# Attention with a mixture of experts on one core: GpSimd's additions in pieces, relus two ahead, unit 1's second weight later, the last tile in two

## Chip, cores and metric

One core of a Trainium2 chip. The number that counts is the device time of one execution, in microseconds (us). The time before is the median of three timed runs; one more execution was profiled, and all rows below are from it.

## What is computed

```python
# q, k, v: (2, 8, 576, 64); hidden 32; moe: N=1152 tokens, D=512, E=4 experts, F=1024
scores = scale * q @ k.T + bias          # bias[h,i,j] = relu(psi*w1 + b1) @ w2, psi = log1p|i-j| / log1p(i)
attn   = softmax(scores)
x      = (attn @ v)  as (1152, 512)
p      = domain_probs / domain_probs.sum(-1)
for e in range(4):
    h    = relu(x @ w1[e])               # 1152 x 1024
    out += p[:, e] * (h @ w2[e])         # 1152 x 512
```

## The kernel before

The attention stage comes first (to about 195 us). It leaves x in SBUF as a sum of two float16 parts (`xx`, high and low), 512 features on 4 x 128 partitions by 1152 tokens. The expert stage cuts the four experts into eight units of 512 hidden columns (`NU = 8`). Each unit has a first weight (512 x 512, `m = 0`) and a second one (`m = 1`). Both are loaded as float32 in halves of 128 x 1024 (`raw`), scaled by a power of two of the largest element, and split into a high and a low float16 part: `whi` (L457, ScalarE; L459 where VectorE does it) and `wlo` (L463, VectorE) for the second weight, L577 and L578 for the first one of units 1 to 7. A product takes three matmuls per 128 rows: high by high, high by low, low by high.

Unit 0 is plain. `mm1` (L475 to L477) makes its hidden rows in three token blocks c of 384 and four column blocks ft of 128; for each, ScalarE applies the relu twice (`ev_a`: L480 into the float32 buffer `hf`, of which there are three, and L481 into the float16 `hh`), and VectorE forms the low part by a difference (`ev_v`, L484). `mm2` (L497 to L499) multiplies a tile of 128 tokens (tau 0 to 8) by the second weight, 12 matmuls of 512 columns, and `sum_up` (L504 for unit 0, L506 for the others) adds it to `acc` by the gate. I write M1.5 for mm2 of unit 1, tile 5.

Units 1 to 7 save one product in eight (seven block products in place of eight, `quad`, L594), for which sums of blocks of x and of the first weight are needed. x is put together in float32 by GpSimd (`x_whole`, L547), summed by VectorE (`x_sums`, L544) and split again (`x_halves`, L555 and L553). The weight's sums are GpSimd's (`w_sums`, L574). Each of a unit's 28 block products goes into one of four PSUM banks; VectorE adds them (L665), ScalarE copies (L685) and applies the relus (L675, L676), GpSimd forms the low part (L677). Tokens come in two pairs of 320 and 256 columns.

The largest element of a weight is found by VectorE per partition (`wmax`, L427, in halves; L436 joins two), written to memory (L439), read back to all partitions (L443) and reduced (`w_red`, L446); `wscale` is five small steps, `gate_unit` (L452) one on 128x9 elements. The outcome goes out tile by tile (`store`, L512, on SP's queue).

The order of all this is set by two planners of the class `Plan`: each step has a priority, an estimated cost, the steps that it needs (`deps`) and steps that must only stand ahead of it (`after`), and the planner writes the instructions in the order of a simulated run. On the chip each engine then takes its own instructions in that order and waits for data alone. The first planner covers the attention stage, unit 0's blocks c = 0 and 1 and the early weights (its steps for unit 1 have names with a 1 at the end, `whi1`, `wlo1`, `gate1`). The second one, `plan_experts`, covers the rest; there `weights(u)` prepares a unit's weights, `second(u, tau)` is mm2 with its sum and store.

Of the kernel before, what the change touches and what calls it, by code (L numbers as in the profile page):

```python
# [155 lines left out]
def tile_attention_moe(ctx: ExitStack, tc: tile.TileContext, qd, kd, vd, cst, ltab, dp, mw1, mw2, out):  # L156
# [328 lines left out]

    def mm2(u, tau, ps):
        if u:
            i = tau // 5
            hh, hl = hpair(i, 0), hpair(i, 1)
            ts = slice(P * (tau - 5 * i), P * (tau - 5 * i) + P)  # L490
        else:
            c, tt = divmod(tau, 3)
            hh, hl = hpart(u, c, 0), hpart(u, c, 1)
            ts = slice(P * tt, P * tt + P)
        wh, wl = wpart(u, 1, 0), wpart(u, 1, 1)
        for ft in range(4):
            T.matmul(ps, hh[:, ft, ts], wh[:, ft], start=(ft == 0), stop=False)  # L497
            T.matmul(ps, hh[:, ft, ts], wl[:, ft], start=False, stop=False)  # L498
            T.matmul(ps, hl[:, ft, ts], wh[:, ft], start=False, stop=(ft == 3))  # L499

    def sum_up(u, tau, ps):
        g, acc = gu[:, u % 2, tau:tau + 1], moe["acc"][:, tau]
# [93 lines left out]
    def plan_experts():  # L596
# [10 lines left out]
        def all_(kind, u, n):  # L607
            return [(kind, u, k) for k in range(n)] if u >= 0 else []

        def weights(u):  # L610
            at = 42.0 * u - 34 if u > 1 else 5.0
            p2, p1 = u - 2, u - 1
            for m in range(2 if u > 1 else 0):
                for j in range(2):
                    if u > 1:
                        after = [("part", p1, k) for k in range(4)] if m == 0 else [("whi", p1, j), ("wlo", p1, j)] if p1 > 1 else []
                        op(("load", u, m, j), "S", at - 10, 1.4, lambda m=m, j=j: load_w(u, m, j), deps=after)
                    prev = (all_("part", p2, 4) + ([("gate", p2)] + [("wlo", p2, k) for k in range(2)] if p2 > 1 else [])) if p2 >= 1 else []
                    op(("wmax", u, m, j), "V", at + 2 * m + j, 1.21, lambda m=m, j=j: wmax(u, m, j), deps=[("load", u, m, j)] if u > 1 else [], after=prev)
                op(("wboth", u, m), "V", at + 2 * m + 2, 0.16, lambda m=m: w_both(u, m), deps=[("wmax", u, m, j) for j in range(2)], after=[("wred", u - 1)] if u > 2 else [])  # L620
# [8 lines left out]
            for k, (c, fns) in enumerate(zip((1.15, 0.63, 0.63, 1.6), w_parts(u))):  # L629
                for e, x, fn in zip("AV", (0, 0.15 * c), fns):  # L630
                    op((("parth" if e == "A" else "part"), u, k), e, at + 12 + 3 * k, c + x, fn, deps=([("wscale", u, 0)] if u > 1 else []) + ([("wsum", u)] if k != 1 else []) + ([("parth", u, k)] if e == "V" else []), after=used)
            if u == 1:
                return
            for j in range(2):
                used2 = [("mm2", p2, tau) for tau in range(NTAU)] if p2 >= 0 else []
                op(("whi", u, j), "A", 42.0 * u - 12 + 4 * j, 1.14, lambda j=j: whi("A", u, 1, j), deps=[("wscale", u, 1)], after=used2)
                op(("wlo", u, j), "V", 42.0 * u - 11 + 4 * j, 1.28, lambda j=j: wlo("V", u, 1, j), deps=[("whi", u, j)])
            op(("gate", u), "V", 42.0 * u - 4, 0.29, lambda: gate_unit(u), deps=[("wscale", u, m) for m in range(2)], after=[("sum", p2, tau) for tau in range(NTAU)] if p2 >= 0 else [])

        def second(u, tau, at):  # L640
# [188 lines left out]
    op("wred1", (), early, w_red, 1, deps=[("wcast1",)])  # L829
    op("gate1", (), early, gate_unit, 1, deps=[("wscale1", 0), ("wscale1", 1), ("prep_gate",)])  # L830
    for c in range(2):
        for ft in range(4):
            for kt in range(4):
# [4 lines left out]
                   deps=[("xlo", 3 * c + i) for i in range(3)] + [("wlo", 0, j) for j in range(2)])  # L838
            op("ev_a", (c, ft), PR["ev"], lambda c=c, ft=ft, key=key: ev_a(0, c, ft, buf[key][:, 0:384], hf[:, (4 * c + ft) % 3]), deps=[("mm1", c, ft, 3)], use=[key], after=[("ev_v", c, ft - 1)] if ft else [("ev_v", c - 1, 3)] if c else [])
# [78 lines left out]
```

## Time and profile before

| | |
|---|---|
| median of three timed runs | 566.19 us (565.79 to 566.46) |
| the profiled execution, its time | 566.17 us |
| its span, first to last instruction | 564.4 us |
| TensorE busy | 542.4 us, 96% |
| VectorE busy | 408.4 us, 72% |
| ScalarE busy | 293.8 us, 52% |
| GpSimd busy | 146.3 us, 26% |
| mean granted TensorE clock | 0.987 of full speed |

Busy time is an average over stages that have different limits, so the table alone doesn't tell what a change is worth. It is to be read by stretches: which engine waits, for whom, and what that one was doing. A row of the timeline has the start, the length, the engine, the line, what is written and read, and in brackets the idle time before it and what ended it.

### The profile page before, as it was taken

The numbers are of one execution on the slowest core, as the hardware profiler recorded it, in microseconds if no ns is written. First come the engines' busy times: TensorE is split into PE (matmuls) and PEld (weight loads), VectorE is DVE, ScalarE is ACT, GpSimd is POOL, SyncE is SP. The second block draws the span as 40 slices with busy tenths as digits, with TensorE's granted clock in tenths as the row PEclk, the third lists the DMA queues.
The fourth block names the chain that finished last, engine by engine and source line by source line (L and its number), as shares of the span: only waits on it lengthen the run. The fifth ranks groups of instructions, "written<-read, shape, count | busy, mean of one in ns | idle before, by whom it ended". The sixth has DMA issues, their size and how long they took to land.

```text
span 564.4 us, 11030 instructions
## 1 busy us (share of the span) xinstructions
PE 542.4 (96%) x4354; PEld 341.4 (60%) x4354; DVE 408.4 (72%) x829; ACT 293.8 (52%) x611; POOL 146.3 (26%) x156
## 2 busy tenths in 40 slices
PE   8769999999999995999999999999999999999997
PEld 3236667777777852547556565665665665565753
DVE  7658887878889496887795976967958957534532
ACT  5568888787787541625534544544334533423410
POOL 0000000000000082007263471371642624322310
PEclk9799999999999997999999999999999999999999
DMA  6984332132441102021041311410312210000022
GB/s 210 235 279 136 105 122 79 62 104 71 138 148 39 11 1 74 1 75 11 14 136 11 115 35 11 149 11 17 135 10 75 75 11 1 2 1 0 1 76 93
DMA packets 22020, 40.63 MB, mean 72 GB/s; under 512 B 3024, under 2 KB 4048, under 8 KB 21968
## 3 DMA queue, kind: packets, MB, share of 16 engines
q1 hardware_dynamic: 21680, 39.33, 23.9%
q8 instruction: 34, 0.56, 0.4%
q10 hardware_dynamic: 288, 0.59, 0.3%
q14 instruction: 18, 0.15, 0.1%
HBM read 25.75 MB, written 2.37 MB: 50 GB/s over the span
## 4 chain that ended last, share of the span: by engine, by line
PE 87%; DVE 5%; DMA 4%; ACT 2%; issue 1%; SPq 0%; ACTq 0%; DVEq 0%
PE bank L594 24%; PE bank L497 11%; PE bank L499 11%; PE bank L498 11%; PE bank L350 7%; PE bank L318 7%; PE bank L335 7%; PE bank L291 5%; PE bank L361 2%; DMA biasA<-obr 1%; DMA biasB<-obr 1%; DVE hh L484 1%; DMA vv<-vd 1%; DVE wb L463 1%; PE bank L231 1%
## 5 line engine op out<-in xcount | busy, mean ns | idle before, releaser
L677 POOL TENSOR_TENSOR hp<-hf,hp 128x320 f16<-128x320 f32 (+1 forms) x112 | 92.1, 838 | 203.4 <-ACT hf L676 202.4
L594 PEld LDWEIGHTS <-wn 128*128 128x128 f16 x1176 | 115.0, 98 | 40.4 <-issue 1.7
L675 ACT ACTIVATE hp<-xsf 128x320 f16<-128x320 f32 (+1 forms) x112 | 49.0, 437 | 137.9 <-DVE xsf L665 137.4
L665 DVE SCALAR_TENSOR_TENSOR xsf<-bank,xsf 128x320 f32<-128x320 f32 (+1 forms) x196 | 82.4, 451 | 25.6 <-PE bank L594 18.4
L594 PE MATMUL bank<-xs,wn 128*128 128x320 f16 (+1 forms) x672 | 98.2, 286 | 1.0 <-ACT xsf L685 0.6
L506 DVE SCALAR_TENSOR_TENSOR acc<-bank,gu,acc 128x512 f32<-128x512 f32 x63 | 47.1, 747 | 66.9 <-PE bank L499 66.9
L594 PE MATMUL bank<-xx,wn 128*128 128x320 f16 (+1 forms) x504 | 75.5, 286 | 0.0
L330 ACT ACTIVATE er<-er,mr 128x576 f32<-128x576 f32 x72 | 55.2, 769 | 10.6 <-DVE mr L326 10.4
L286 DVE TENSOR_SCALAR fr<-lt,npt 128x576 f32<-128x576 f32 x117 | 52.9, 514 | 5.7 <-PE bank L291 5.4
L497 PE MATMUL bank<-wb,hp 128*128 128x512 f16 x144 | 54.6, 379 | 0.0
L498 PE MATMUL bank<-wb,hp 128*128 128x512 f16 x144 | 54.6, 379 | 0.0
L499 PE MATMUL bank<-wb,hp 128*128 128x512 f16 x144 | 54.6, 379 | 0.0
L318 PE MATMUL bank<-ks,qr 64*128 64x288 f32 (+1 forms) x320 | 47.2, 427 | 5.1 <-ACT obr L294 2.4
L291 PE MATMUL bank<-fr,cs 128*32 128x288 f32 x576 | 44.4, 434 | 3.8 <-ACT obr L294 3.2
L676 ACT ACTIVATE hf<-xsf 128x320 f32<-128x320 f32 (+1 forms) x112 | 47.8, 427 | 0.2 <-POOL hp L677 0.2
L339 ACT ACTIVATE etr<-bank 128x512 f32<-128x512 f32 x69 | 37.5, 596 | 16.6 <-PE bank L335 15.3
L350 PE MATMUL bank<-etr,vv 128*64 128x128 f32 (+1 forms) x800 | 45.5, 265 | 0.0
L350 PEld LDWEIGHTS bank<-etr,vv 128*64 128x64 f32 x800 | 39.6, 137 | 8.6 <-issue 6.8
L499 PEld LDWEIGHTS <-hp 128*128 128x128 f16 x252 | 24.7, 98 | 29.7
L335 PE MATMUL bank<-ident,er 128*128 128x128 f32 x324 | 42.1, 278 | 0.0
L335 PEld LDWEIGHTS bank<-ident,er 128*128 128x128 f32 x324 | 34.8, 141 | 12.0 <-issue 8.4
L497 PE MATMUL bank<-wa,hp 128*128 128x512 f16 x108 | 40.9, 379 | 0.0
(104 smaller groups left out, 763.8 us busy)
## 6 DMA issues: line engine op xcount, KB each, us to landing
raw<-mw SPq DMA_DIRECT2D x32, 512.0 KB
biasB<-obr SPq DMA_DIRECT2D x32, 144.0 KB
biasA<-obr SPq DMA_DIRECT2D x32, 144.0 KB
vv<-vd SPq DMA_DIRECT2D x8, 320.0 KB
ks<-kd SPq DMA_DIRECT2D x8, 288.0 KB
qr<-qd SPq DMA_DIRECT2D x9, 256.0 KB
biasA<-obr SPq DMA_DIRECT2D x8, 288.0 KB
out<-acc SPq DMA_DIRECT2D x8, 256.0 KB
```

Source lines behind the costliest of these rows:

```text
L286: ENG[e].tensor_scalar(out=f, in0=src, scalar1=npt[:, g:g + 1], scalar2=None, op0=ALU.max)
L291: T.matmul(buf["pb", n][32 * t:32 * t + 32, half, 0:288], W2, buf["f", n, t][:, 288 * half:288 * half + 288], start=True, stop=True)
L318: T.matmul(s_out(2 * p + h, c0, c1, half), q[r, c0:c1], ks[r, HP * b + hp, 288 * half:288 * half + 288], start=True, stop=True)
L330: A.activation(out=ehalf(u), in_=ehalf(u), func=AF.Exp, scale=-1.0, bias=buf["m", u // 2][:, u % 2:u % 2 + 1], accum_out=buf["sum", tau][: ...
L335: T.transpose(buf["t", tau, g][:, P * i:P * i + P], buf["e", HP * tau + hp][:, P * j:P * j + P], ident)
L350: T.matmul(x[64 * h:64 * h + 64, P * hp + c0:P * hp + c1], vv[:, HP * b + hp, 5 * h + i], buf["et", tau, g][:, P * j + c0:P * j + c1], sta ...
L497: T.matmul(ps, hh[:, ft, ts], wh[:, ft], start=(ft == 0), stop=False)
L498: T.matmul(ps, hh[:, ft, ts], wl[:, ft], start=False, stop=False)
L499: T.matmul(ps, hl[:, ft, ts], wh[:, ft], start=False, stop=(ft == 3))
L594: T.matmul(ps, w[lw][:, k], x[:, lx, k], start=k == 0 and lw + lx == 0, stop=k == 1 and lw == 1)
L665: V.scalar_tensor_tensor(out=tmp(name), in0=ps(a), scalar=2.0 ** -HS, in1=tmp(other), op0=ALU.mult, op1=ALU.add)
L677: op(("lo", u, i, x), "G", at + pos + EV, 0.2 + 0.6 * r, lambda: G.tensor_tensor(out=lo, in0=buf[f][:, 0:n], in1=hi, op=ALU.subtract), dep ...
```

## The change

Four edits, three of them in what the planners are told.

GpSimd's `x_whole` is cut along the four feature blocks: per token pair four instructions in place of one. In the first planner the relu pair of a block need no longer stand behind the difference just before it, but behind the one before that (a pair may be up to two ahead). Unit 1's `whi`, `wlo` and `gate_unit` leave the first planner and are made by `weights(1)` in the second one, always by ScalarE and VectorE; mm2 of unit 1 and loads of later units are told of them. The last tile's mm2, sum and store are done in two parts, of 320 and 192 columns.

```diff
-    def x_whole(i):
-        G.tensor_tensor(out=moe["xf"][:, :, tokens(i)], in0=xx[:, 0, :, tokens(i)], in1=xx[:, 1, :, tokens(i)], op=ALU.add)
+    def x_whole(i, k):
+        G.tensor_tensor(out=moe["xf"][:, k, tokens(i)], in0=xx[:, 0, k, tokens(i)], in1=xx[:, 1, k, tokens(i)], op=ALU.add)
...
-                        after = [("part", p1, k) for k in range(4)] if m == 0 else [("whi", p1, j), ("wlo", p1, j)] if p1 > 1 else []
+                        after = [("part", p1, k) for k in range(4)] if m == 0 else [("whi", p1, j), ("wlo", p1, j)]
...
-                    prev = (all_("part", p2, 4) + ([("gate", p2)] + [("wlo", p2, k) for k in range(2)] if p2 > 1 else [])) if p2 >= 1 else []
+                    prev = ([("gate", p2)] + all_("part", p2, 4) + [("wlo", p2, k) for k in range(2)]) if p2 >= 1 else []
...
-            if u == 1:
-                return
...
         def second(u, tau, at):
             i = tau // 5
+            if (u, tau) == (NU - 1, NTAU - 1):
+                for k, o in enumerate((slice(0, 320), slice(320, DM))):
+                    key = (u, tau, k)
+                    op(("mm2",) + key, "T", at, 1.3, lambda o=o, key=key: mm2(u, tau, buf[("o",) + key], o), ...
+                    op(("sum",) + key, "V", at + 2.6 + EV, 0.45, lambda o=o, key=key: sum_up(u, tau, buf[("o",) + key], o), ...
+                    op(("store",) + key, "S", at, 0.5, lambda o=o: store(tau, o), deps=[("sum",) + key])
+                return
             if u:
-                deps = [("lo", u, i, k) for k in range(8)] + ([("wlo", u, j) for j in range(2)] if u > 1 else [])
+                deps = [("lo", u, i, k) for k in range(8)] + [("wlo", u, j) for j in range(2)]
...
-            op(("xw", i), "G", 6.0 * i, 6.0 - i, lambda i=i: x_whole(i))
+            for k in range(4):
+                op(("xw", i, k), "G", 6.0 * i, 1.4 - 0.2 * i, lambda i=i, k=k: x_whole(i, k))
...
-            if m:
-                op("whi1", (j,), early, whi, 1, m, j, choice=True, deps=[("wscale1", m)])
-                op("wlo1", (j,), early, wlo, "V", 1, m, j, deps=[("whi1", j)])
...
-    op("gate1", (), early, gate_unit, 1, deps=[("wscale1", 0), ("wscale1", 1), ("prep_gate",)])
...
-            op("ev_a", (c, ft), ..., after=[("ev_v", c, ft - 1)] if ft else [("ev_v", c - 1, 3)] if c else [])
+            op("ev_a", (c, ft), ..., after=[("ev_v",) + divmod(4 * c + ft - 2, 4)] if 4 * c + ft > 1 else [])
```

What that does to the order is seen on VectorE at two places. The first is behind the scales of unit 1, while TensorE ends unit 0's first products (L484 are the differences, L452 the gate step, L459 and L463 unit 1's second weight, L504 unit 0's sums). Before:

```order
L452 TENSOR_SCALAR gu<-gate,ws 128x9
L484 TENSOR_TENSOR hh<-hf,hh 128x384
L459 TENSOR_SCALAR wb<-raw_1669,ws 128x1024
L463 SCALAR_TENSOR_TENSOR wb<-raw_1669,ws,wb 128x1024
L484 TENSOR_TENSOR hh<-hf,hh 128x384
L463 SCALAR_TENSOR_TENSOR wb<-raw_1669,ws,wb 128x1024
L484 TENSOR_TENSOR hh<-hf,hh 128x384 x4
```

Now, at the same place (L544 is a sum of x, L579 was L578):

```order
L484 TENSOR_TENSOR hh<-hf,hh 128x384 x6
L504 TENSOR_SCALAR acc<-bank,gu 128x512
L452 TENSOR_SCALAR gu<-gate,ws 128x9
L463 SCALAR_TENSOR_TENSOR wb<-raw_1669,ws,wb 128x1024
L504 TENSOR_SCALAR acc<-bank,gu 128x512
L544 TENSOR_TENSOR xsf<-xsf 128x2x320
L579 SCALAR_TENSOR_TENSOR wn<-raw,ws,wn 128x512
L504 TENSOR_SCALAR acc<-bank,gu 128x512
L544 TENSOR_TENSOR xsf<-xsf 128x2x320
L463 SCALAR_TENSOR_TENSOR wb<-raw_1669,ws,wb 128x1024
```

The six differences now stand in a row, and the second weight and the gate step have gone behind unit 0's first sum. On ScalarE eight relu pairs stand in a row in the same way; L457, which stood behind the third pair, comes twice behind the eighth.

The second place is the border from unit 1 to unit 2 on VectorE, behind unit 2's scales (L506 sums of unit 1, L578 and L463 unit 2's weights, L665 additions of unit 1). Before:

```order
L578 SCALAR_TENSOR_TENSOR wn<-raw,ws,wn 128x1024
L506 SCALAR_TENSOR_TENSOR acc<-bank,gu,acc 128x512
L578 SCALAR_TENSOR_TENSOR wn<-raw,ws,wn 128x512 x2
L506 SCALAR_TENSOR_TENSOR acc<-bank,gu,acc 128x512
L463 SCALAR_TENSOR_TENSOR wa<-raw_1669,ws,wa 128x1024
L578 SCALAR_TENSOR_TENSOR wn<-wt,ws,wn 128x1536
L665 SCALAR_TENSOR_TENSOR xsf<-bank,xsf 128x256 x3
```

Now (L579 was L578, L672 was L665):

```order
L579 SCALAR_TENSOR_TENSOR wn<-raw,ws,wn 128x1024
L463 SCALAR_TENSOR_TENSOR wa<-raw_1669,ws,wa 128x1024
L672 SCALAR_TENSOR_TENSOR xsf<-bank,xsf 128x256 x3
L506 SCALAR_TENSOR_TENSOR acc<-bank,gu,acc 128x512
L579 SCALAR_TENSOR_TENSOR wn<-raw,ws,wn 128x512 x2
L672 SCALAR_TENSOR_TENSOR xsf<-bank,xsf 128x256
L506 SCALAR_TENSOR_TENSOR acc<-bank,gu,acc 128x512
L579 SCALAR_TENSOR_TENSOR wn<-wt,ws,wn 128x1536
```

The last piece of unit 2's first weight (128x1536) has moved behind the four last additions of unit 1. Ahead of this place, unit 2's maxima of the second weight (L427 on raw_1669) have moved from unit 0's sums into unit 1's additions, and the step that reduces them (L446) from the first half of unit 1's last additions to behind two L506. On TensorE M1.5 now stands ahead of unit 2's first product, where it stood behind its fourth.

## Rows read from the trace of the kernel before

**Rows 1.** Stretch, length, busy us (count) of PE, PEld, DVE, ACT, POOL, clock, DMA, GB/s.
```profile
251.50:530.00 278.50, 277.51 (x1761) 172.09 (x1760) 199.76 (x380) 122.09 (x271) 116.41 (x128) 1.00 0.16 42
```

**Rows 2.** Waits, 196 to 222 us: who for whom, total us, times, longest.
```profile
ACT hf L480 <- DVE hh L484: 7.5, 3, 4.6
...
PE bank L497 <- ACT hh L481: 6.7, 1, 6.7
```

**Rows 3.** VectorE: all L484 (ns min/median/max); timeline start, length (us).
```profile
L484 DVE TENSOR_TENSOR hh<-hf,hh x12: 543/551/3906, 199.0 to 237.6; 128x384 f16<-128x384 f32 x12
...
200.96 3.91 DVE L484 TENSOR_TENSOR hh<-hf,hh 128x384 f16<-128x384 f32 x1 [0.24 <-ACT hh L481]
...
205.60 3.22 DVE L452 TENSOR_SCALAR gu<-gate,ws 128x9 f32<-128x9 f32 x1
```

**Rows 4.** GpSimd, timeline from 199 us.
```profile
199.32 9.47 POOL L547 TENSOR_TENSOR xsf<-xx 128x2560 f32<-128x2560 f16 x2 [9.91 <-DVE xx L380]
...
208.75 1.65 POOL L574 TENSOR_TENSOR wt<-raw 128x512 f32<-128x512 f32 x1
```

**Rows 5.** ScalarE, timeline, 205 to 218 us.
```profile
205.54 1.15 ACT L457 ACTIVATE wb<-raw,ws 128x1024 f16<-128x1024 f32 x1 [2.66 <-DVE ws L271]
...
217.47 0.49 ACT L480 ACTIVATE hf<-bank 128x384 f32<-128x384 f32 x1 [1.80 <-DVE hh L484]
...
217.85 0.48 ACT L481 ACTIVATE hh<-bank 128x384 f16<-128x384 f32 x1
```

**Rows 6.** TensorE, timeline: around the pause, and unit 1's first product.
```profile
211.39 0.33 PE L477 MATMUL bank<-xx,wa 128*128 128x384 f16 x1
...
218.39 0.59 PE L497 MATMUL bank<-wa,hh 128*128 128x512 f16 x1 [6.67 <-ACT hh L481]
...
251.50 0.98 PE L594 MATMUL bank<-xx,wn 128*128 128x320 f16 x6
```

**Rows 7.** Stretches, columns as in rows 1.
```profile
40.00:42.00 2.00, 0.15 (x6) 0.01 (x2) 2.00 (x5) 0.00 (x0) 0.00 (x0) 1.00 0.79 300
...
215.00:215.50 0.50, 0.00 (x0) 0.00 (x0) 0.50 (x1) 0.50 (x2) 0.50 (x1) 1.00 0.97 332
...
218.00:222.00 4.00, 3.61 (x9) 1.31 (x9) 0.87 (x2) 0.94 (x2) 0.00 (x0) 0.50 0.40 130
...
222.00:226.00 4.00, 4.00 (x19) 1.72 (x17) 2.77 (x4) 0.00 (x0) 0.00 (x0) 0.94 0.00 0
```

**Rows 8.** Units 1 and 2: timelines of VectorE and SP's queue; one chain row.
```profile
247.53 1.81 DVE L578 SCALAR_TENSOR_TENSOR wn<-wt,ws,wn 128x1536 f16<-128x1536 f32 x1
...
259.90 0.34 SPq L439 DMA_DIRECT2D wd<-wx  x1
...
263.35 0.34 SPq L443 DMA_DIRECT2D wg<-wd  x1
...
268.03 0.41 DVE L446 TENSOR_REDUCE ws<-wg 128x2 f32<-128x256 f32 x1
...
272.90 0.75 DVE L506 SCALAR_TENSOR_TENSOR acc<-bank,gu,acc 128x512 f32<-128x512 f32 x1 [2.17 <-PE bank L499]
...
275.49 0.75 DVE L506 SCALAR_TENSOR_TENSOR acc<-bank,gu,acc 128x512 f32<-128x512 f32 x1
...
276.16 1.41 DVE L578 SCALAR_TENSOR_TENSOR wn<-raw,ws,wn 128x512 f16<-128x512 f32 x2
...
279.94 1.81 DVE L578 SCALAR_TENSOR_TENSOR wn<-wt,ws,wn 128x1536 f16<-128x1536 f32 x1
...
284.54 3.92 PE bank L594 x30
```

**Rows 9.** Groups by form (count, busy us, mean ns, idle); one stretch.
```profile
L506 DVE SCALAR_TENSOR_TENSOR acc<-bank,gu,acc 128x512 f32<-128x512 f32 x63 | 47.1, 747 | 66.9 <-PE bank L499 66.9
...
L665 DVE SCALAR_TENSOR_TENSOR xsf<-bank,xsf 128x256 f32<-128x256 f32 x98 | 37.5, 416 | 8.9 <-PE bank L594 4.8 <-ACT xsf L685 3.6
...
562.00:563.00 1.00, 0.00 (x0) 0.00 (x0) 0.00 (x0) 0.00 (x0) 0.00 (x0) 1.00 0.70 262
```

More of the change, by code (lines that the diff above doesn't have):

```diff
@@ L496, in mm2, with sum_up @@
         for ft in range(4):
[L497 to L502, printed above, removed]
+            T.matmul(ps[:, o], hh[:, ft, ts], wh[:, ft, o], start=(ft == 0), stop=False)
+            T.matmul(ps[:, o], hh[:, ft, ts], wl[:, ft, o], start=False, stop=False)
+            T.matmul(ps[:, o], hl[:, ft, ts], wh[:, ft, o], start=False, stop=(ft == 3))
+    def sum_up(u, tau, ps, o=slice(0, DM)):
+        g, acc, ps = gu[:, u % 2, tau:tau + 1], moe["acc"][:, tau, o], ps[:, o]
         if u == 0:
@@ L506, in sum_up, with store @@
             V.scalar_tensor_tensor(out=acc, in0=ps, scalar=g, in1=acc, op0=ALU.mult, op1=ALU.add)
-    def store(tau):
-        acc = moe["acc"][:, tau]
+    def store(tau, o=slice(0, DM)):
+        acc = moe["acc"][:, tau, o]
         if tau:
             r = (tau - 1) % 2 * S + (tau - 1) // 2 * P
-            SP.dma_start(out=out[r:r + P], in_=acc)
+            SP.dma_start(out=out[r:r + P, o], in_=acc)
         else:
@@ L631, in weights @@
                     op((("parth" if e == "A" else "part"), u, k), e, at + 12 + 3 * k, c + x, fn, deps=([("wscale", u, 0)] if u > 1 else []) + ([("wsum", u)] if k != 1 else []) + ([("parth", u, k)] if e == "V" else []), after=used)
-            if u == 1:
-                return
             for j in range(2):
                 used2 = [("mm2", p2, tau) for tau in range(NTAU)] if p2 >= 0 else []
-                op(("whi", u, j), "A", 42.0 * u - 12 + 4 * j, 1.14, lambda j=j: whi("A", u, 1, j), deps=[("wscale", u, 1)], after=used2)
+                op(("whi", u, j), "A", 42.0 * u - 12 + 4 * j, 1.14, lambda j=j: whi("A", u, 1, j), deps=[("wscale", u, 1)] if u > 1 else [], after=used2)
                 op(("wlo", u, j), "V", 42.0 * u - 11 + 4 * j, 1.28, lambda j=j: wlo("V", u, 1, j), deps=[("whi", u, j)])
-            op(("gate", u), "V", 42.0 * u - 4, 0.29, lambda: gate_unit(u), deps=[("wscale", u, m) for m in range(2)], after=[("sum", p2, tau) for tau in range(NTAU)] if p2 >= 0 else [])
+            op(("gate", u), "V", 42.0 * u - 4, 0.29, lambda: gate_unit(u), deps=[("wscale", u, m) for m in range(2)] if u > 1 else [], after=[("sum", p2, tau) for tau in range(NTAU)] if p2 >= 0 else [])
         def second(u, tau, at):
             i = tau // 5
+            if (u, tau) == (NU - 1, NTAU - 1):
+                for k, o in enumerate((slice(0, 320), slice(320, DM))):
+                    key = (u, tau, k)
+                    op(("mm2",) + key, "T", at, 1.3, lambda o=o, key=key: mm2(u, tau, buf[("o",) + key], o), deps=[("lo", u, i, x) for x in range(8)] + [("wlo", u, j) for j in range(2)] + ([("mm2", u, tau - 1)] if not k else [("mm2", u, tau, 0)]), new=[("o", ("o",) + key)])
+                    op(("sum",) + key, "V", at + 2.6 + EV, 0.45, lambda o=o, key=key: sum_up(u, tau, buf[("o",) + key], o), deps=[("mm2",) + key, ("gate", u)], use=[("o",) + key], after=[("sum", u - 1, tau)])
+                    op(("store",) + key, "S", at, 0.5, lambda o=o: store(tau, o), deps=[("sum",) + key])
+                return
             if u:
-                deps = [("lo", u, i, k) for k in range(8)] + ([("wlo", u, j) for j in range(2)] if u > 1 else [])
+                deps = [("lo", u, i, k) for k in range(8)] + [("wlo", u, j) for j in range(2)]
             else:
@@ L646, in second @@
             op(("mm2", u, tau), "T", at, 2.6, lambda: mm2(u, tau, buf["o", u, tau]), deps=deps, new=[("o", ("o", u, tau))])
-            op(("sum", u, tau), "V", at + 2.6 + EV, 0.75, lambda: sum_up(u, tau, buf["o", u, tau]), deps=[("mm2", u, tau)] + ([("gate", u)] if u > 1 else []), use=[("o", u, tau)], after=[("sum", u - 1, tau)] if u else [])
+            op(("sum", u, tau), "V", at + 2.6 + EV, 0.75, lambda: sum_up(u, tau, buf["o", u, tau]), deps=[("mm2", u, tau)] + ([("gate", u)] if u else []), use=[("o", u, tau)], after=[("sum", u - 1, tau)] if u else [])
             if u == NU - 1:
@@ L699, in plan_experts @@
         for i in range(2):
-            op(("xw", i), "G", 6.0 * i, 6.0 - i, lambda i=i: x_whole(i))
+            for k in range(4):
+                op(("xw", i, k), "G", 6.0 * i, 1.4 - 0.2 * i, lambda i=i, k=k: x_whole(i, k))
             for k, fn in enumerate(x_sums(i)):
-                op(("xs", i, k), "V", 1 + 12.0 * i + k, 0.85, fn, deps=[("xs", i, k - 1)] if k else [("xw", i)])
+                op(("xs", i, k), "V", 1 + 12.0 * i + k, 0.85, fn, deps=[("xs", i, k - 1)] if k else [("xw", i, x) for x in range(4)])
             for a in range(2):
@@ L838, in tile_attention_moe @@
                    deps=[("xlo", 3 * c + i) for i in range(3)] + [("wlo", 0, j) for j in range(2)])
[L839 removed]
+            op("ev_a", (c, ft), PR["ev"], lambda c=c, ft=ft, key=key: ev_a(0, c, ft, buf[key][:, 0:384], hf[:, (4 * c + ft) % 3]), deps=[("mm1", c, ft, 3)], use=[key], after=[("ev_v",) + divmod(4 * c + ft - 2, 4)] if 4 * c + ft > 1 else [])
             op("ev_v", (c, ft), PR["ev"], lambda c=c, ft=ft: ev_v(0, c, ft, None, hf[:, (4 * c + ft) % 3]), deps=[("ev_a", c, ft)])
```

4 lines of the change are left out of this document (2 added, 2 removed).

## Prediction

> **What bounds the kernel now.** I read the table of stretches first. Behind 251.50 us, in the expert stage, TensorE is busy 277.51 of 278.50 us [rows 1]: there only a shorter product or a shorter end could help, and nothing in the change shortens a product. The list of waits then names the one large hole, at the border from unit 0's first products to its second ones: TensorE waits 6.7 us for a relu on ScalarE, and ScalarE itself waits 7.5 us, in three pieces, for VectorE's differences (L484) [rows 2]. So the question is why a difference is late. Its median is 0.551 us, its longest 3.906 us; that one runs from 200.96 to 204.87 [rows 3]. GpSimd's two additions of L547 cover 199.32 to 208.79 [rows 4]; shared out by columns (2560 and 2048) the first ends near 204.6. VectorE's gate step on 128x9 elements starts at 205.60 and ends at 208.82 [rows 3], which is where the second addition ends. My reading is that VectorE stands still until GpSimd's running instruction is over, and then gets its turn.
>
> ScalarE's order adds to it: L457 (unit 1's second weight) stands between relus and waits 2.66 us for a scale that is queued on VectorE behind the long difference, and the last relu pair waits 1.80 us for a difference [rows 5]. Its second relu ends at 218.33, and TensorE's first L497 starts at 218.39 [rows 5, 6]. TensorE had nothing to do since 211.72 (211.39 + 0.33), hence 6.67 us.
>
> **What the clock adds.** After that pause the clock is lower: 1.00 up to 215.50, 0.50 from 218 to 222, 0.94 on average from there to 226 [rows 7]. A shorter hole, 40 to 42 us with TensorE busy 0.15 us, left it at 1.00 [rows 7]. Of the two levels (1.2 and 2.4 GHz) TensorE ran at the lower one for 3.61 us (218.39 to 222) and 4 x 0.06 / 0.5 = 0.48 us, so 4.09 us in which half the work was done: 2.05 us lost.
>
> **The change, part by part.** *GpSimd's additions.* Two instructions become eight. The 9.47 us shared out by columns give 1.32 us for a piece of 640 and 1.05 for one of 512, if nothing is paid per instruction; the nearest short row, 1.65 us for 512 columns beside VectorE's steps [rows 4], gives up to 2.1 us for 640. So a difference now waits for one piece, at most 1.3 to 2.1 us, in place of up to 3.4.
>
> The Trainium skill ("SBUF — State Buffer", "Who interferes with whom") says that an operation of VectorE with both inputs in SBUF and a GpSimd instruction that reads SBUF exclude each other for a whole instruction, whoever starts first. The long difference above agrees. By the same rule VectorE holds up GpSimd as well, which speaks against many small pieces: each can be put off by a difference, and the sums of x come later.
>
> That cost has a cover. Eight differences take 8 x 0.55 = 4.4 us, so the pieces end near 199.3 + 9.5 + 4.4 = 213.2, and the first sum of x stands on VectorE behind two sum_ups of unit 0, which come some 5 us later. Cost taken: zero; with pieces at the upper price up to 1 us, since 8 x 0.5 us more still end before 218.
>
> *Relus two ahead, weights later.* Now ScalarE has eight relu pairs in a row, and a pair needs only the difference three before it (three buffers hf). TensorE ends the last group at 211.72, and the pair for it needs the fifth difference. Even if GpSimd gave VectorE no turn before all eight pieces are done (208.8), four more differences of 0.55 end at 211.0, in time; so TensorE alone releases the last pair. The two relus take 0.86 us (217.47 to 218.33 [rows 5]); with 0.1 us for the handovers TensorE goes on at 212.7. The pause falls from 6.67 to 0.97 us: **-5.70**. It can't vanish, because L497's bank is the one that the last pair reads. With pieces at the upper price it is 1.5 us.
>
> *Clock.* A pause of 0.97 us is shorter than the hole that left the clock alone: **-2.05**; at the other end of the bound, 0.
>
> *Up to unit 1's products.* VectorE loses two maxima (L427) and the cast L459 in this stretch and gains two L463 and the gate step; each but the last is one pass over 1024 columns, so its work stays about as long. ScalarE gets two casts of 1.15 us [rows 5] where it mostly waits. Before, VectorE's last piece of the weights ended at 249.34 [rows 8] and TensorE came at 251.50 [rows 6]: 2.2 us of cover, and both ends move with TensorE. GpSimd's L574 now falls beside the gate step and the first L463: at most two waits of 1.65 us, so 3.3 - 2.2 = 1.1 us at the worst. Cost taken: zero.
>
> *Border to unit 2.* Two maxima now stand between unit 1's additions, the pair of L436 comes seven additions later, and the last piece of unit 2's weights stands behind two more sum_ups and one more addition. I count from unit 1's first product (251.50). Before: M1.0's sum_up starts at 272.90 (+21.4), the next one 2.59 us later, the last piece runs to 281.75 (+30.3), and unit 2's products start behind unit 1's last one of 0.65 us, at 285.2 (+33.7) [rows 8]. After: by the count of additions the maxima are sent near +14.5; L443 follows 3.45 us later (as 263.35 follows the send at 259.90) and lands no more than 4.7 us after that (263.35 to 268.03 [rows 8]), so by +22.7. w_red stands behind the second sum_up, at +24.7, and doesn't wait. Behind it come its own 0.4, two scales of 0.6 (five small steps, what is left between 272.90 and 276.16 beside two sum_ups and a piece), a sum_up 0.7, a piece and L463 of 1.3 each, three additions 1.2, a sum_up, two pieces 1.4: about +33. The last addition waits for TensorE, +33.9, then a sum_up 0.75 and the last piece 1.8: +36.6. TensorE does M1.5 first (2.6 us, to +36.3), a product of 0.8 us, and wants the piece some 0.3 us into the next, at +37.4. Cover 0.8 us, thin. Cost taken: zero; up to 2.5 us.
>
> From unit 3 on the two orders differ by a place here and there, at the same distance to the products: zero.
>
> *End.* The last tile's 12 matmuls of 512 columns become 12 of 320 and 12 of 192, by columns the same. Its last sum_up works on 192 columns: 747 ns for 512 and 416 for 256 [rows 9] give about 0.34, so -0.41. The last store carries 98 of 262 KB; the full one moved in 1.0 us [rows 9]. In proportion that is -0.63, at a fixed price 0; I take half, -0.3, and +0.1 for TensorE's 12 more weight loads (0 to 0.35). Sum **-0.6**, from -1.0 to 0.
>
> The Trainium skill ("DMA: Bandwidth & Descriptors", "Bandwidth") advises few large transfers and shows small ones ruled by a fixed cost. No row here shows a store of 98 KB. By that advice the store saves nothing and the sum is 0.3 us higher.
>
> **Sum.** 5.70 + 2.05 + 0.6 = 8.35 us off the profiled execution's 566.17 us (span 564.4). The median of the three timed runs, 566.19, is the same. Forecast 557.8 us.
>
> **Rivals.** *A, unit 2's weights come late.* VectorE's queue ahead of the last piece is 0.8 us from deciding. For: one wait for a GpSimd instruction of 1.65 us would do. Against: VectorE waits for TensorE several times in that stretch, and these waits absorb lateness. Price 0.5 to 2.5 us, with 1.5: 559.3 us. *B, it doesn't do what it says*: relus and differences still take turns, the pause stays above 3 us and the clock falls all the same. Gain then at most 3.7 + 0.6, so about 562 us. Against stands the count above, in which even eight unbroken pieces don't put off the last relu. *C, slower.* The copy of the maxima to all partitions (L439, L443, w_red) leaves later, and w_red stands in VectorE's queue ahead of all that unit 2 needs; the additions behind it hold TensorE's four banks, so TensorE stops with it. It costs from a landing at +24.7 on, 2 us behind the latest by the trace. To undo 8.35 us and add 1.1, it must land 11 us later than that: over 567.3 us. Nothing in the trace points there.
>
> **How the numbers follow.** The forecast 0.74 (556.8 to 558.8), A 0.16, B 0.05, C 0.03, and 0.02 for a gain within 0.2%. The range runs from the best end of the tail, with the two small holes left in the expert stage closing a little, 556.8, to the upper part of A, 560.6. 0.2%, or 1.1 us, is about what a measurement here can tell from no change. Faster 0.95, same 0.02, slower 0.03.
>
> **What the next profile would show.** A pause of about 1 us before the first L497, released by a relu; clock 1.00 through it; the longest difference under 2.7 us; eight additions of GpSimd of 1.0 to 2.1 us; unit 1's products from about 243.7; no hole in TensorE at unit 2's first products; a last sum_up near 0.34 us. I am wrong if the pause stays above 2 us, if the clock reads 0.5 behind it, or if TensorE waits at unit 2 for the last piece of its weights.

## The result and the profile after

The changed kernel took 559.86 us (median of four runs, 559.28 to 561.29), against 566.24 us for the kernel before in the same comparison: a ratio of 0.9892, 95% interval 0.9873 to 0.9912. The forecast was 557.8 us in a range of 556.8 to 560.6. The direction and the range held; the forecast itself was 2 us too low, and what that was made of is told under "Right and wrong". The profiled execution took 559.86 us, with a span of 558.1 us and a mean clock of 0.991.

In the changed kernel L548 is GpSimd's addition (L547 before), L575 the weights' sums (L574), L579 the low part of the first weight (L578), L595 the products (L594), L672 the additions of products (L665), L692 their copies on ScalarE (L685), L683 the relu that GpSimd's difference reads, and L684 that difference (L677). Lines with numbers under 547 have kept them.

The list of waits of TensorE from 205 to 560 us (who for whom, total us, times, longest):

```profile
PE bank L499 <- POOL hp L684: 1.1, 1, 1.1
PE bank L497 <- ACT hh L481: 1.0, 1, 1.0
PE bank L595 <- ACT xsf L692: 0.6, 2, 0.3
PE bank L595 <- DVE xsf L672: 0.4, 2, 0.2
```

Against [rows 2] the wait of 6.7 us has shrunk to 1.0, and the first line is new. The last two were there before, at the same size. The timeline of TensorE at both stops and at unit 1's first product (start us, length, what, idle before and who ended it):

```profile
213.60 0.38 PE L497 MATMUL bank<-wa,hh 128*128 128x512 f16 x1 [0.96 <-ACT hh L481]
...
244.71 0.98 PE L595 MATMUL bank<-xx,wn 128*128 128x320 f16 x6
...
281.83 0.39 PE L499 MATMUL bank<-wb,hp 128*128 128x512 f16 x1 [1.06 <-POOL hp L684]
```

The first answers to [rows 6]: a pause of 0.96 us where 6.67 stood. The clock around it, by stretches (columns as in rows 1), answers to [rows 7]: 1.00 where 0.50 and 0.94 stood.

```profile
211.70:215.00 3.30, 2.34 (x13) 1.14 (x12) 1.97 (x2) 2.32 (x4) 3.22 (x4) 1.00 0.00 0
218.00:222.00 4.00, 4.00 (x21) 1.87 (x20) 3.41 (x5) 0.00 (x0) 0.00 (x0) 1.00 0.38 131
222.00:226.00 4.00, 4.00 (x27) 2.43 (x25) 4.00 (x6) 1.40 (x4) 0.00 (x0) 1.00 0.10 16
```

VectorE's longest difference and GpSimd's additions, to be read beside [rows 3, 4]: 3.91 us has become 1.64, and two additions of together 9.47 us have become eight of together 11.60.

```profile
201.88 1.64 DVE L484 TENSOR_TENSOR hh<-hf,hh 128x384 f16<-128x384 f32 x1 [0.24 <-ACT hh L481]
```

```profile
200.25 11.60 POOL L548 TENSOR_TENSOR xsf<-xx 128x640 f32<-128x640 f16 x8 [9.91 <-DVE xx L380]
```

**Where the new stop comes from.** It is the last product of M1.5 at the border to unit 2. GpSimd forms the last low part that M1.5 reads; VectorE works on the 128x1536 piece of unit 2's weights meanwhile. First GpSimd's last two rows, then VectorE's:

```profile
277.19 1.57 POOL L684 TENSOR_TENSOR hp<-hf,hp 128x256 f16<-128x256 f32 x2 [12.20 <-ACT hf L683]
279.70 2.08 POOL L684 TENSOR_TENSOR hp<-hf,hp 128x256 f16<-128x256 f32 x1 [0.94 <-ACT hf L683]
```

```profile
279.44 1.81 DVE L579 SCALAR_TENSOR_TENSOR wn<-wt,ws,wn 128x1536 f16<-128x1536 f32 x1
281.17 1.69 DVE L463 SCALAR_TENSOR_TENSOR wa<-raw,ws,wa 128x1024 f16<-128x1024 f32 x1
```

The piece ends at 281.25, GpSimd's difference at 281.78, and TensorE goes on at 281.83. In the kernel before the same difference took 0.67 us, since the piece was over by then, and M1.5 stood behind four products of unit 2:

```profile
286.49 0.67 POOL L677 TENSOR_TENSOR hp<-hf,hp 128x256 f16<-128x256 f32 x1 [0.95 <-ACT hf L676]
```

What the stop costs is read from unit 1's and 2's sums (L506). Here are the first one after, then the fourteenth, which is behind the border, before and after:

```profile
266.12 0.75 DVE L506 SCALAR_TENSOR_TENSOR acc<-bank,gu,acc 128x512 f32<-128x512 f32 x1 [2.17 <-PE bank L499]
```

```profile
329.46 0.74 DVE L506 SCALAR_TENSOR_TENSOR acc<-bank,gu,acc 128x512 f32<-128x512 f32 x1
```

```profile
323.90 0.74 DVE L506 SCALAR_TENSOR_TENSOR acc<-bank,gu,acc 128x512 f32<-128x512 f32 x1
```

The first one starts at 272.90 before [rows 8] and at 266.12 after, 6.78 us earlier. The fourteenth starts 5.56 us earlier. So 1.22 us are given back there, and from the fourteenth to the last sum of a whole tile nothing more.

**The end.** The last tile's two sums, and the stretches behind them, all from the changed kernel:

```profile
554.05 0.55 DVE L506 SCALAR_TENSOR_TENSOR acc<-bank,gu,acc 128x320 f32<-128x320 f32 x1 [0.88 <-PE bank L499]
555.04 0.42 DVE L506 SCALAR_TENSOR_TENSOR acc<-bank,gu,acc 128x192 f32<-128x192 f32 x1 [0.44 <-PE bank L499]
```

```profile
555.00:556.00 1.00, 0.00 (x0) 0.00 (x0) 0.42 (x1) 0.00 (x0) 0.00 (x0) 1.00 0.47 164
556.00:557.00 1.00, 0.00 (x0) 0.00 (x0) 0.00 (x0) 0.00 (x0) 0.00 (x0) 1.00 0.31 98
```

The last sum took 0.42 us in place of 0.75. From its end to the end of the span it is 2.64 us (555.46 to 558.1), against 3.09 before (561.31 to 564.4).

**A measure free of the attention stage.** The first L484 starts at 199.01 us in the profile before [rows 3] and at 199.93 after, though the instructions ahead of it are the same. In the profiles of the experiments it lies between 199.31 and 199.90. The rows show where that comes from: one product of the attention stage (L318), before and after.

```profile
48.17 1.24 PE L318 MATMUL bank<-ks,qr 64*128 64x288 f32 x8 [0.81 <-DVE sr L354]
```

```profile
49.09 1.24 PE L318 MATMUL bank<-ks,qr 64*128 64x288 f32 x8 [1.95 <-DMA qr<-qd]
```

From this row to the first L484 it is 150.84 us in both, and in the profiles of the experiments too, to 0.01 us. In the kernel before, the load of q was there in time; in the nine other profiles TensorE waits for it, and the row starts between 48.47 and 49.09. In e5, which has the instructions of the kernel before up to 212 us, it starts at 48.92. So that variation belongs to the executions, not to the change; why the load lands at different times stays open. Therefore below I compare from the start of the first L484 to the end of the span: **365.39 us before, 358.17 after, 7.22 less.** The span is given to 0.1 us, so such a difference is good to about 0.1 us. Of the sums in between, the same ones agree within 0.02 us from one kernel to another where nothing was changed.

### The profile page after: what moved, and what is told of

Same layout as the page of the kernel before. It is cut to its first block, busy times and chain, and to the rows that moved or that the text cites. A ratio compares the mean times of both kernels' runs of the same rounds, so it can differ in the third digit from the quotient of the medians.

```text
span 558.1 us, 11067 instructions
## 1 busy us (share of the span) xinstructions
PE 541.3 (97%) x4366; PEld 341.9 (61%) x4366; DVE 402.1 (72%) x829; ACT 295.0 (53%) x612; POOL 146.1 (26%) x162
## 4 chain that ended last, share of the span: by engine, by line
PE 88%; DMA 5%; ACT 3%; DVE 1%; issue 1%; POOL 1%; SPq 1%; ACTq 0%; POOLq 0%
PE bank L595 24%; PE bank L499 10%; PE bank L497 10%; PE bank L498 10%; PE bank L350 7%; PE bank L318 7%; PE bank L335 7%; PE bank L291 5%; PE bank L361 2%; PE bank L475 1%; DMA qr<-qd 1%; PE bank L477 1%; PE bank L476 1%; DMA biasB<-obr 1%; DMA biasA<-obr 1%
## 5 line engine op out<-in xcount | busy, mean ns | idle before, releaser
L684 POOL TENSOR_TENSOR hp<-hf,hp 128x320 f16<-128x320 f32 (+1 forms) x112 | 91.0, 827 | 197.2 <-ACT hf L683 194.9
L595 PEld LDWEIGHTS <-wn 128*128 128x128 f16 x1176 | 115.1, 98 | 40.5 <-issue 1.7
L672 DVE SCALAR_TENSOR_TENSOR xsf<-bank,xsf 128x320 f32<-128x320 f32 (+1 forms) x196 | 82.3, 452 | 24.2 <-PE bank L595 17.3
L595 PE MATMUL bank<-xs,wn 128*128 128x320 f16 (+1 forms) x672 | 98.0, 286 | 1.0 <-ACT xsf L692 0.6
L506 DVE SCALAR_TENSOR_TENSOR acc<-bank,gu,acc 128x512 f32<-128x512 f32 (+1 forms) x64 | 47.3, 739 | 66.7 <-PE bank L499 66.6
L595 PE MATMUL bank<-xx,wn 128*128 128x320 f16 (+1 forms) x504 | 75.5, 286 | 0.0
L499 PE MATMUL bank<-wb,hp 128*128 128x512 f16 (+2 forms) x148 | 55.2, 373 | 1.1 <-POOL hp L684 1.1
L497 PE MATMUL bank<-wb,hp 128*128 128x512 f16 (+2 forms) x148 | 55.2, 373 | 0.0
L498 PE MATMUL bank<-wb,hp 128*128 128x512 f16 (+2 forms) x148 | 55.2, 373 | 0.0
L318 PE MATMUL bank<-ks,qr 64*128 64x288 f32 (+1 forms) x320 | 46.5, 427 | 5.4 <-ACT obr L294 3.1
L291 PE MATMUL bank<-fr,cs 128*32 128x288 f32 x576 | 45.7, 445 | 3.8 <-ACT obr L294 3.2
L683 ACT ACTIVATE hf<-xsf 128x320 f32<-128x320 f32 (+1 forms) x112 | 47.8, 427 | 0.0
L497 PE MATMUL bank<-wa,hp 128*128 128x512 f16 x108 | 40.9, 379 | 0.0
```

The lines of the kernel that those rows point to most:

```text
L291: T.matmul(buf["pb", n][32 * t:32 * t + 32, half, 0:288], W2, buf["f", n, t][:, 288 * half:288 * half + 288], start=True, stop=True)
L318: T.matmul(s_out(2 * p + h, c0, c1, half), q[r, c0:c1], ks[r, HP * b + hp, 288 * half:288 * half + 288], start=True, stop=True)
L497: T.matmul(ps[:, o], hh[:, ft, ts], wh[:, ft, o], start=(ft == 0), stop=False)
L498: T.matmul(ps[:, o], hh[:, ft, ts], wl[:, ft, o], start=False, stop=False)
L499: T.matmul(ps[:, o], hl[:, ft, ts], wh[:, ft, o], start=False, stop=(ft == 3))
L595: T.matmul(ps, w[lw][:, k], x[:, lx, k], start=k == 0 and lw + lx == 0, stop=k == 1 and lw == 1)
```

## The experiments

The theory is a sum: the pause, the clock that falls behind it, the new stop at the border, and the end. Each of the four terms has a run of its own, and the last run puts three cures together. e1 to e4 ran on one chip (the kernel before there: 566.91 us) and e5 to e8 on another (566.15 us); each ratio is against these. The changed kernel was not timed again there, so an experiment is compared with it by the traces. Where a sum (L506) is said to come earlier or later, it is counted from the first L484 of the same profile.

**The relus two ahead.** This edit was not run, because there is nothing to run. The changed kernel written with the old rule for the relu pairs is the same program, instruction for instruction on every engine and with the same waits; and so is the old kernel written with the new rule. The edit does nothing by itself.

**e1, the kernel before with the eight pieces alone.**

```diff
-        G.tensor_tensor(out=moe["xf"][:, :, tokens(i)], in0=xx[:, 0, :, tokens(i)], in1=xx[:, 1, :, tokens(i)], op=ALU.add)
+        G.tensor_tensor(out=moe["xf"][:, k, tokens(i)], in0=xx[:, 0, k, tokens(i)], in1=xx[:, 1, k, tokens(i)], op=ALU.add)
```

> The kernel before with GpSimd's additions in eight pieces and nothing else of the change. Theory: VectorE waits for one running GpSimd instruction, so the longest difference (L484) falls from 3.9 to under 2.5 us, but unit 1's second weight still stands between relus and differences; the pause ahead of the first L497 falls from 6.7 to about 3.3 us (2.5 to 4.5), and the time to 561 to 563.5 us. Rival (the order of ScalarE and VectorE alone makes the pause, pieces don't matter): pause 5.5 us or more, time 565 to 566.5 us.

Measured: 561.77 us (560.32 to 563.71), ratio 0.9906 (0.9885 to 0.9927). The longest difference falls to 1.63 us, the pause to 2.48 us, and unit 1's sums come 4.50 us earlier than in the kernel before. But the clock did fall, and only when TensorE was back at work. The first L497, then the stretches:

```profile
215.09 0.38 PE L497 MATMUL bank<-wa,hh 128*128 128x512 f16 x1 [2.48 <-ACT hh L481]
```

```profile
214.00:215.00 1.00, 0.00 (x0) 0.00 (x0) 1.00 (x2) 0.84 (x3) 1.00 (x1) 1.00 0.73 268
215.00:216.00 1.00, 0.91 (x4) 0.39 (x4) 1.00 (x2) 0.64 (x2) 0.92 (x2) 0.88 0.59 225
216.00:219.00 3.00, 3.00 (x8) 1.03 (x7) 2.69 (x2) 0.00 (x0) 2.92 (x3) 0.50 0.00 0
219.00:220.00 1.00, 1.00 (x5) 0.43 (x4) 0.44 (x1) 0.00 (x0) 0.81 (x1) 0.91 0.00 0
```

0.12 + 3 x 0.50 + 0.09 = 1.71 us are lost to the clock in this execution. There is no stop at M1.5 here, as TensorE's order is the old one.

**e2, the changed kernel with the two long additions.**

```diff
-        G.tensor_tensor(out=moe["xf"][:, k, tokens(i)], in0=xx[:, 0, k, tokens(i)], in1=xx[:, 1, k, tokens(i)], op=ALU.add)
+        G.tensor_tensor(out=moe["xf"][:, :, tokens(i)], in0=xx[:, 0, :, tokens(i)], in1=xx[:, 1, :, tokens(i)], op=ALU.add)
```

> The changed kernel with GpSimd's two long additions whole again. Theory: with eight relu pairs in a row and the weight behind them, the fifth difference is done before the last pair even if two of the differences wait for a whole addition (up to 4 us each); the pause stays at 1.0 to 1.5 us, the clock at 1.00, and the time within 0.5 us of the changed kernel's 559.9. Rival (the pieces carry the gain): pause above 3 us, time above 562 us.

Measured: 560.15 us (559.89 to 560.38), ratio 0.9879 (0.9859 to 0.9899). The long difference is back (3.91 us), and yet the pause is only 1.59 us and the clock 1.00:

```profile
201.29 3.91 DVE L484 TENSOR_TENSOR hh<-hf,hh 128x384 f16<-128x384 f32 x1 [0.24 <-ACT hh L481]
```

```profile
213.64 0.38 PE L497 MATMUL bank<-wa,hh 128*128 128x512 f16 x1 [1.59 <-ACT hh L481]
```

Unit 1's sums lie 0.63 us behind those of the changed kernel, which is the difference of the pauses, 1.59 - 0.96. In the changed kernel unit 1's first sum comes 6.78 + 0.92 = 7.70 us earlier, counted from the first L484. So moving unit 1's second weight and gate step out of the way carries nearly all of that gain, 7.70 - 0.63 = 7.07 us; which of the two steps matters more was not tested. The pieces alone carry 4.50 us (e1), and only 0.63 beside the move: what they cure, the move cures nearly all by itself.

**e3, the changed kernel with the last tile whole** (the branch for the last tile in `second` taken out).

> The changed kernel with the last tile in one part again. Theory: from the start of the last tile's matmuls to the end of the span 6.63 us as before in place of 5.88, so 0.75 us more time, about 560.6 us. Rival (the smaller store saves nothing, only the shorter sum does): 0.3 us more.

Measured: 560.51 us (559.60 to 562.26), ratio 0.9885 (0.9865 to 0.9904). From the first L484 to the end it is 358.90 us, 0.73 more than in the changed kernel. All sums ahead of the last agree within 0.01 us, so the end is worth 0.73 us and touches nothing else.

**e4, unit 2's piece of 128x1536 in three of 128x512**, so that GpSimd's difference can come between.

```diff
+    def w_thirds(u):
+        for i in range(3):
+            hi, lo = (moe["wn"][:, u % 2, l, 512 * (T1 + i):512 * (T1 + i) + 512] for l in range(2))
+            V.scalar_tensor_tensor(out=lo, in0=moe["wt"][:, 512 * i:512 * i + 512], scalar=wcol(u, 0, 5), in1=hi, op0=ALU.mult, op1=ALU.subtract)
```

> The changed kernel with VectorE's last piece of unit 2's first weight (128x1536) in three instructions of 128x512. Theory: GpSimd's last difference of unit 1, 2.08 us long in the changed kernel, waits for that one VectorE instruction; with thirds it takes 0.67 to 1.4 us, TensorE's stop of 1.06 us ahead of M1.5's last matmul falls under 0.4 us, and the time by 0.7 to 1.2 us to about 559. Rival (the difference is late because M1.5 stands right behind unit 1's last product, whatever VectorE does): stop 0.8 us or more, time unchanged.

Measured: 559.53 us (558.92 to 559.62), ratio 0.9864 (0.9847 to 0.9882). The stop at M1.5 is down to 0.16 us (its last two matmuls start at 279.95 and 280.32, usually 0.21 apart), as GpSimd's last difference takes 1.01 us in place of 2.08. But from the first L484 to the end it is 358.21 us, no less than before the cure, and not the 0.7 to 1.2 us less that were expected. Two new waits stand behind it, at unit 2's first products (L600 are the products here, L677 the additions, L689 GpSimd's difference, L592 the thirds). GpSimd, TensorE and VectorE, each in a view of its own:

```profile
279.25 1.01 POOL L689 TENSOR_TENSOR hp<-hf,hp 128x256 f16<-128x256 f32 x1 [0.94 <-ACT hf L688]
```

```profile
285.10 0.97 PE L600 MATMUL bank<-xx,wn 128*128 128x320 f16 x6 [0.32 <-DVE xsf L677]
286.62 0.97 PE L600 MATMUL bank<-xs,wn 128*128 128x320 f16 x6 [0.55 <-DVE xsf L677]
```

```profile
278.99 2.48 DVE L592 SCALAR_TENSOR_TENSOR wn<-wt,ws,wn 128x512 f16<-128x512 f32 x3
281.40 1.27 DVE L463 SCALAR_TENSOR_TENSOR wa<-raw,ws,wa 128x1024 f16<-128x1024 f32 x1
282.59 0.28 DVE L452 TENSOR_SCALAR gu<-gate,ws 128x9 f32<-128x9 f32 x1
282.79 1.20 DVE L427 TENSOR_REDUCE ws<-raw 128x1 f32<-128x1024 f32 x1
283.92 0.73 DVE L506 SCALAR_TENSOR_TENSOR acc<-bank,gu,acc 128x512 f32<-128x512 f32 x1
284.58 0.47 DVE L677 SCALAR_TENSOR_TENSOR xsf<-bank,xsf 128x320 f32<-128x320 f32 x1
284.98 1.20 DVE L427 TENSOR_REDUCE ws<-raw 128x1 f32<-128x1024 f32 x1
286.10 2.46 DVE L677 SCALAR_TENSOR_TENSOR xsf<-bank,xsf 128x320 f32<-128x320 f32 x6
```

VectorE works without a gap there, and two of unit 3's maxima (L427), which nobody needs yet, stand ahead of additions that TensorE's banks wait for. By these rows the border has two limits, one behind the other; e7 and e8 test that.

**e5, the kernel before with the pause filled.**

```diff
+        for _ in range(24):
+            T.matmul(bank[:, 0], xx[:, 0, 0, 0:128], xx[:, 0, 0, 0:512], start=True, stop=True)
```

> The kernel before, with 24 matmuls of 128x512 (their results are never read) put on TensorE between unit 0's first products and its second ones, where it waited 6.67 us. Nothing else moves, so relus and differences end when they did. Theory (the clock falls because TensorE stands still): 24 x 0.22 us fill 5.2 of the 6.67 us, a pause of about 1.5 us is left, as long as the 1.59 us that left the clock at 1.00, and the clock stays at 1.00 behind it. From the first L484 to the end of the span 365.39 - 2.05 = 363.3 us, and the time 2 us below the kernel before. Rival (the clock falls here for something else, the start of unit 0's second products or the load of the other engines): 0.50 behind the pause as before, time unchanged, 365.4 us.

Measured: 564.47 us (564.08 to 564.94), ratio 0.9971 (0.9961 to 0.9982). From the first L484 to the end it is 363.44 us, 1.95 less than before. Real work starts as late as it did; only the clock is different:

```profile
219.15 0.38 PE L497 MATMUL bank<-wa,hh 128*128 128x512 f16 x1 [1.51 <-ACT hh L481]
```

```profile
218.00:222.00 4.00, 2.85 (x14) 1.31 (x14) 1.69 (x5) 1.48 (x3) 0.00 (x0) 1.00 0.39 131
222.00:226.00 4.00, 4.00 (x20) 1.82 (x19) 3.95 (x5) 0.00 (x0) 0.00 (x0) 1.00 0.00 0
```

So it was TensorE's idle time that made the clock fall, and that fall cost 1.98 us (the sums of unit 1 come earlier by that much). The executions that were not traced agree: the mean clock is 0.989 to 0.994 in the seven of e5 and 0.984 to 0.987 in the eleven of the kernel before beside them. The rival, another cause at that place, is out.

**e6, the changed kernel with another order of banks.**

```diff
-o=[bank[:, i] for i in (6, 7, 3, 2)]
+o=[bank[:, i] for i in (3, 2, 6, 7)]
```

> The changed kernel with the PSUM banks for unit 0's second products handed out in the order 3, 2, 6, 7 in place of 6, 7, 3, 2, so that the first of them doesn't get the bank that the last relu pair still reads. Theory (the 0.96 us that are left of the pause are the wait for that bank and nothing else): pause below 0.2 us, from the first L484 to the end of the span 358.17 - 0.9 = 357.3 us, about 559.0 us. Rival (TensorE then waits for the relus' data or VectorE's difference, or a later product takes over the wait for the bank): pause or a new wait of 0.5 to 0.9 us at the next products, 358.0 us and the time unchanged.

Measured: 558.23 us (557.49 to 558.56), ratio 0.9859 (0.9845 to 0.9872). The first L497 follows the last L477 with no idle time at all, and the sums come 1.12 us earlier than in the changed kernel (357.00 us from the first L484 to the end, expected 357.3), more than the 0.96 us that the trace gave for the wait. The rows show why:

```profile
211.99 0.33 PE L477 MATMUL bank<-xx,wa 128*128 128x384 f16 x1
212.15 0.38 PE L497 MATMUL bank<-wa,hh 128*128 128x512 f16 x1
```

A matmul of 384 columns is written down with 0.33 us, but the next one starts 0.16 us after it. A stop costs what lies between two starts, 213.60 - 212.32 - 0.16 = 1.12 us in the changed kernel; the idle time in brackets begins later, at the modelled end. The stop at M1.5 reads 1.06 us and costs 1.22 in the same way.

**e7, the changed kernel with unit 3's maxima behind unit 2's first seven additions.**

```diff
-after=prev)
+after=prev + ([("add", 2, 0, 0, "c12")] if u == 3 else []))
```

> The changed kernel, with unit 3's four maxima (L427, 1.2 us each, on VectorE) put behind the first seven additions of unit 2. Theory (at the border to unit 2 two limits lie one behind the other: first GpSimd's last difference for M1.5, held up by VectorE's 128x1536 piece, then VectorE's queue, in which these maxima stand): taking away the second one alone leaves the stop of 1.0 to 1.1 us at M1.5 where it is, and from the first L484 to the end of the span it stays 358.2 us (357.9 to 358.5). Rival (the maxima are the whole reason, and the difference is late for them): the stop is gone and 357.0 us.

Measured: 558.49 us (558.35 to 558.81), ratio 0.9866 (0.9853 to 0.9879), and 357.45 us from the first L484 to the end, 0.72 us less than expected. That number alone would have spoken for the rival (357.0), but at the border the theory held: the stop is there with the same 1.06 us, GpSimd's difference takes 2.08 us, and the fourteenth sum lies where it lay in the changed kernel. What I had not expected comes some 110 us behind that sum. The move also changes the planner's order of the units behind, and one of the two pairs of small waits that are in both kernels (L595 for L672 and for L692, at 435 us) is gone:

```profile
PE bank L499 <- POOL hp L684: 1.1, 1, 1.1
PE bank L497 <- ACT hh L481: 1.0, 1, 1.0
PE bank L595 <- ACT xsf L692: 0.3, 1, 0.3
PE bank L595 <- DVE xsf L672: 0.2, 1, 0.2
```

From 470 us on all sums come 0.69 us earlier. Which instruction's new place closed that hole I did not test.

**e8, thirds, later maxima and bank order together.**

> The changed kernel with three edits together: unit 2's piece of 128x1536 in three of 128x512, unit 3's maxima behind unit 2's first seven additions, and the banks 3, 2, 6, 7 for unit 0's second products. Theory: no stop at M1.5, no wait of unit 2's first products for VectorE's additions, pause below 0.2 us: 358.17 - 1.2 - 0.9 = 356.1 us from the first L484 to the end of the span, about 557.7 us. Rival (something else is next behind VectorE's queue, GpSimd's sums of the weights or ScalarE's copies): only the 0.9 us of the banks, 357.3 us, about 559.0 us.

Measured: 556.35 us (556.16 to 556.65), ratio 0.9828 (0.9815 to 0.9842): faster than the kernel before and, by the trace, than the changed one. TensorE's list of waits from 205 to 560 us has only the last of the small ones left:

```profile
PE bank L600 <- ACT xsf L697: 0.3, 1, 0.3
PE bank L600 <- DVE xsf L677: 0.2, 1, 0.2
```

From the first L484 to the end it is 355.29 us, 2.88 less than the changed kernel: 2.19 at the fourteenth sum, as the theory said (2.1), and the 0.69 us from 435 us that e7 showed as well. The border by itself, from the fourteenth sum's start counted from the first L484, in the changed kernel 123.97 us:

| | fourteenth sum | against the changed kernel |
|---|---|---|
| e4, thirds alone | 124.08 | +0.11 |
| e7, maxima later alone | 123.97 | 0.00 |
| e6, banks alone | 122.85 | -1.12 |
| e8, all three | 121.78 | -2.19 |

Thirds and maxima are worth nothing one by one, and -2.19 + 1.12 = -1.07 us together, which is the stop's 1.22 us less the 0.16 that thirds leave.

## Right and wrong, step by step

| step | forecast, us | measured, us | by |
|---|---|---|---|
| pause ahead of the first L497 | -5.70 | -5.71 (6.67 to 0.96) | profile after |
| clock behind it | -2.05 | -1.98 | e5; profile after: 1.00 throughout |
| up to unit 1's products | 0 | -0.02 (31.11 against 33.11 - 1.98) | profile after |
| border to unit 2 | 0, up to +2.5 | +1.22 | L506 rows; e4, e7, e8 |
| end | -0.6 (-1.0 to 0) | -0.74 | profile after; e3 -0.73 |
| sum | -8.35 | -7.22 | first L484 to end |

The sum of the measured steps, -5.71 - 1.98 - 0.02 + 1.22 - 0.74 = -7.23, agrees with the 7.22 us of the whole. Between the two profiled executions only 6.31 us arrive (566.17 to 559.86), and 6.38 between the medians. The 0.92 us that the profiles lack are the later first L484, a load that landed late and no step of the change; for the medians no trace shows it.

So 559.86 us misses the band that the prediction gave to its forecast (556.8 to 558.8) and lies in the part of the range that was there for rival A. That it came near A's 559.3 is luck: 1.22 us of border and 0.92 us of a late load, neither of which is A's reason.

**The step that failed** is "Border to unit 2 ... Cover 0.8 us, thin. Cost taken: zero". The count behind it followed the last piece of the weights, and the piece was in time: counted to end at +36.6, it ended at +36.54 (281.25 - 244.71), and TensorE never waited for it. (The steps listed there add up to +32.3, not +33; nothing hangs on it.) The count did not follow what that piece does to its neighbour: GpSimd's last difference for M1.5 took 2.08 us beside it in place of 0.67, and TensorE stood for 1.22 us. The prediction had the mechanism in hand, that a VectorE operation with two inputs and a GpSimd instruction exclude each other. It weighed VectorE holding up GpSimd for the additions only, and at the border the other direction only. Nor does an engine wait for data alone, as the account of the kernel has it. The order printed ahead of the prediction showed both halves of the new stop: the piece now last behind the additions, and M1.5 now ahead of unit 2's products, so that GpSimd's last difference has no slack. The first half is shown by e4 and e8; the second is read from the order, and no run put M1.5 back. Rival A had the place and nearly the size (1.5 us), but another reason, weights that come late.

The Trainium skill ("SBUF — State Buffer", "Who interferes with whom") says that whichever of the two starts first keeps the shared ports for its whole instruction. The rows agree, in both directions: a difference of VectorE took 3.91 us beside GpSimd's long addition (e2; median in the kernel before 0.551), and one of GpSimd took 2.08 us beside VectorE's piece that had begun 0.26 us earlier; with the piece in thirds it took 1.01 us (e4).

**The pause** was right to 0.01 us, for a reason that was half right. The eight relu pairs in a row come from moving the second weight, not from the rule for the relus, which does nothing. And the pieces came first in the account of the cure; e2 shows that they add 0.63 us to the move's 7.07.

**The clock** was right in size. That a short pause leaves it alone was argued from one hole; the runs add pauses of 0.96, 1.51 and 1.59 us with 1.00 behind them, and one of 2.48 us behind which it fell, each from one traced kernel.

**The end** was right within its bounds. The sum gave 0.33 us (forecast 0.41), the store 0.45 (forecast 0.3, half of the proportional 0.63), and what is left for TensorE's additional weight loads is 0.04 us (forecast 0.1, for which no row was given). That the store saves nothing was read too strictly out of the Trainium skill's advice of few large transfers ("DMA: Bandwidth & Descriptors", "Bandwidth"): the section's table has 0.95 us for 64 KB and 6.15 us for 1 MB, for loads, so its times grow with size as well. The 0.45 us measured lie nearer to the proportional end.

**Rival B** (the pause stays) is out by the pause of 0.96 us, and **rival C** (a late copy of the maxima) by TensorE's list of waits, in which no additions are waited for at the border to unit 2; the two waits for L672 are at 435 and 480 us.

## What to carry over

When an operation moves, follow not only whether its result is in time but also what its engine shuts out while it runs: here a VectorE piece that TensorE never waited for stopped it by way of GpSimd. Where two limits lie one behind the other, taking away either gains nothing (e4 +0.11, e7 0.00, together -1.07 us), so a cure that changes nothing is not yet refuted; read who waits next. And price a stop between the starts of two matmuls, not by the idle time in brackets, which was short by 0.16 us each time.

## What was unexpected of the hardware

In e1's profile the clock fell behind a pause of 2.48 us, and not in the pause but after TensorE was back at work: 1.00 in the whole of 214 to 215, with TensorE idle, and 0.50 from 216 to 219 with TensorE busy throughout (e1). In the kernel before it had fallen while TensorE still stood:

```profile
215.00:216.00 1.00, 0.00 (x0) 0.00 (x0) 1.00 (x1) 0.67 (x2) 0.82 (x1) 0.82 0.93 338
216.00:217.00 1.00, 0.00 (x0) 0.00 (x0) 1.00 (x2) 0.00 (x0) 0.00 (x0) 0.50 0.13 49
```

So a pause that ends with the clock at 1.00 is not yet free of that price.

Nor does the same program pay it in each execution. The six executions of e1 took 560.32 to 563.71 us at mean clocks of 0.994 down to 0.985. In the one with 0.994 some 0.006 x 558.5 = 3.4 us of clock are missing in all, as in e2's profile (0.994), where the clock fell in the attention stage alone; so by this estimate it did not fall behind the pause there. The attention stage itself, with the same instructions in all kernels, shows the same: from 28 to 40 us the clock stays at 1.00 in the profile of the kernel before and falls to 0.50 for a time in the nine others. One profile is thin evidence for how long a pause may last.
